# Full-height row loads, a second DMA queue for the first V, and matmuls of zeros at the start of an attention-and-MLP kernel

## The chip, the cores and the metric

The kernel runs on one core of a Trainium2 chip. The metric is the device time of one execution in microseconds (us). The kernel before takes 330.28 us, the median of 5 runs (329.52 to 330.59). One execution of each kernel was taken with a profile: its span (first to last instruction) is about 1.7 us shorter than its device time, and all times of day below are counted from the start of that span.

Engines are named as in the profile: PE multiplies matrices (PEld is its weight load), ACT evaluates functions, DVE and POOL work elementwise, SP only issues DMAs here. POOL and SP each issue DMAs into a queue of their own.

## The reference, cut to what matters

```python
# q, k, v: [B=8, H=8, S=576, D=64] f32
scores = (q @ k.T) / sqrt(D) + slope[h] * -|i - j|       # ALiBi
scores = where((i >= j) & (i - j < 128), scores, -1e9)   # causal window of 128
x = softmax(scores) @ v            # -> x: [B*S = 4608, H*D = 512]
h = x @ w_in                       # w_in:  [512, 2048]
g = h * cos(h)
out = g @ w_out                    # w_out: [2048, 512], out f32
```

The kernel computes in bf16 with f32 accumulation. V, the rows of Q and K, and both weights are f32 in memory. POOL's queue rounds them to bf16 on the way (a casting DMA). What comes through SP's queue in these kernels stays as it is in memory, so V stays f32 there.

## The kernel before

A list scheduler inside the program decides at build time in which order each engine runs its operations; nothing is decided at run time. Batch 0 has a path of its own. Rows of Q and K are loaded in two halves per tensor (`pl` is 0 or 1), transposed by PE through an identity, evicted (copied out of the memory that PE writes) by ACT and DVE; then come pairs of score blocks, exps, a multiplication by a mask that holds window and ALiBi bias, products with V (`pv`), a normalisation, and the first product with w_in for that chunk, with its cosine.

```python
def load_qk(which, src, b, pl):            # two DMAs of 64 partitions each
    fns = []
    for g in range(2):
        fns.append(lambda e, g=g: e.dma_start(
            qB[which][64 * g:64 * g + 64, 2 * pl:2 * pl + 2, :],
            src[b, 4 * g + 2 * pl:4 * g + 2 * pl + 2, :, :].rearrange(
                "h (s j) d -> s h (j d)", j=9)))
    op("pool", fns, w=[("qB", which, pl)], ...)

def load_v(b, order=range(NBLK)):          # NBLK = 5 blocks of up to 128 rows
    for t in order:
        rows = 128 if t < 4 else 64
        op("pool", [lambda e, t=t, rows=rows: e.dma_start(
            vp[b % 2][0:rows, t, :, 0:64],
            v[b, :, 128 * t:128 * t + rows, :].rearrange("h p d -> p h d"))], ...)

# ... the order at the start, which is also POOL's order ...
for pl in range(2):
    load_qk("q", q, 0, pl)
    load_qk("k", k, 0, pl)
    if pl == 0:
        constants()                        # dif, ident: on POOL
load_v(0)
masks()                                    # eight 128x512 exps on ACT
# ... transposes of batch 0 ...
for u in range(4):
    load_w_in(u)                           # 512 of 2048 columns each
for pl in range(2):
    load_qk("q", q, 1, pl)                 # batch 1
    load_qk("k", k, 1, pl)
for u in range(4):
    load_w_out(u)
load_v(1, (3, 4, 0, 1, 2))
attention(0)
```

`r=` and `w=` of an `op` are the data that it reads and writes; the waits follow from them.

The softmax here doesn't subtract the row's maximum and nothing guards it: scores larger than these inputs give would overflow.

Of the kernel before, what the change touches and what calls it, by code (L numbers as in the profile page):

```python
# [34 lines left out]
class Plan:  # L35
# [51 lines left out]

    def schedule(self):
        free = {e: 0 for e in ENG}
        wire = self.WIRE0  # L90
        mode, table = 0, None
        tables = sorted({o.table for o in self.all if o.table is not None})
        left = {t: sum(o.table == t for o in self.all) for t in tables}
        avail = []

        def reach(o, e):
            t = 0
            for d, data in o.preds.items():
                if data == ORDER or self.held(d, data, e):
                    t = max(t, d.start + d.occ)  # L100
                elif d.dma is None and d.eng[0] == e:
                    t = max(t, d.end + 28)
                else:
                    t = max(t, d.end + (53 if e == "pe" else 36))
            return t
        for o in self.all:
            if o.npred == 0:
                avail.append(o)
        order = []
        while avail:  # L110
            phase = next((t for t in tables if left[t]), None)
            best = None
            for e in ENG:
                cand = []
                for o in avail:
                    if e not in o.eng or (o.table is not None and o.table != phase):
                        continue
                    st = max(free[e], reach(o, e))
                    if e == "pe" and o.mode != mode:
                        st += self.SWITCH  # L120
                    cand.append((st, o))
                if not cand:
                    continue
                soon = min(st for st, _ in cand)
                slack = 100 if e == "pe" else 40
                st, o = min(((st, o) for st, o in cand if st <= soon + slack),
                            key=lambda c: (c[1].pri, c[1].seq))
                key = (st, o.pri, o.seq)
                if best is None or key < best[0]:
                    best = (key, e, o)  # L130
            (st, _, _), e, o = best
            avail.remove(o)
            if o.table is not None and o.table != table:
                st += self.TABLE
            if len(o.eng) > 1:
                o.fn, o.occ, o.lat = o.fn[e], o.occ[e], o.lat[e]
                o.eng = (e,)
            o.start = st
            free[e] = st + o.occ
            if o.dma is not None:  # L140
                wire = max(wire, st + 2300) + o.lat
                o.end = max(wire, st + o.occ + 1400) + 500
            else:
                o.end = st + o.lat
            if e == "pe":
                mode = o.mode
            if o.table is not None:
                table = o.table
                left[o.table] -= 1
            order.append(o)  # L150
            for s in o.succs:
                s.npred -= 1
                if s.npred == 0:
                    avail.append(s)
        assert len(order) == len(self.all)
        self.span = max(o.end for o in order)
        self.order = sorted(order, key=lambda o: o.start)
        rank = {id(o): i for i, o in enumerate(order)}
        self.order.sort(key=lambda o: (o.start, rank[id(o)]))
# [81 lines left out]
def bass_alibi_sliding__then__act_gcu_kernel(  # L241
# [8 lines left out]
    with ExitStack() as ctx:  # L250
# [28 lines left out]
        ident = sb("ident", [128, 128])  # L279
        halfpi = sb("halfpi", [128, 1], F32)  # L280
        dif = sb("dif", [128, 2, 128], F32)

        ps = ctx.enter_context(nc.psum_tensor("ps", [128, 8, 512], F32))
        BPE = 2
# [21 lines left out]


        def load_qk(which, src, b, pl):
            fns = []
            for g in range(2):  # L310
                fns.append(lambda e, g=g: e.dma_start(  # L311
                    qB[which][64 * g:64 * g + 64, 2 * pl:2 * pl + 2, :],
                    src[b, 4 * g + 2 * pl:4 * g + 2 * pl + 2, :, :].rearrange(
                        "h (s j) d -> s h (j d)", j=9)))
            op("pool", fns, w=[("qB", which, pl)], dma=f"ld{which}{pl}", occ=1250, lat=1450)

        def load_v(b, order=range(NBLK)):
            for t in order:
# [42 lines left out]

        def constants():
            sel = ["sel"]
            op("pool", lambda e: e.iota(dif[:, :, :], pattern=[[128, 2], [-1, 128]], base=-128,
                                        channel_multiplier=1,
                                        allow_small_or_imprecise_dtypes=True),
               w=["dif"] + sel, occ=350)
            op("pool", lambda e: e.affine_select(
                dif[:, 0, :], dif[:, 0, :], pattern=[[-1, 128]], compare_op=ALU.is_ge,
                fill=-1.0e6, base=-1, channel_multiplier=1), r=["dif"], w=["dif"] + sel, occ=350)  # L370
            op("pool", lambda e: e.affine_select(
                dif[:, 1, :], dif[:, 1, :], pattern=[[1, 128]], compare_op=ALU.is_ge,
                fill=-1.0e6, base=0, channel_multiplier=-1), r=["dif"], w=["dif"] + sel, occ=350)
            op("pool", lambda e: e.memset(ident[:, :], 1.0), w=["ident"] + sel)
            op("pool", lambda e: e.affine_select(
                ident[:, :], ident[:, :], pattern=[[1, 128]], compare_op=ALU.is_equal,
                fill=0.0, base=0, channel_multiplier=-1), r=["ident"], w=["ident"] + sel)
            for i in range(2):
                op("dve", lambda e, i=i: e.memset(vp[i][:, :, :, 64:65], 1.0), w=[("vinit", i)])
                op("dve", lambda e, i=i: e.memset(vp[i][64:128, 4, :, 0:64], 0.0), w=[("vinit", i)])  # L380
                op("dve", lambda e, i=i: e.memset(Pt[i][:, 1024:1088], 0.0), w=[("Pt", i)])
            op("dve", lambda e: e.memset(halfpi[:, :], math.pi / 2.0), w=["halfpi"])
            for i in range(2):
                op("dve", lambda e, i=i: e.memset(
                    tr["k"][i][:, :].rearrange("p (k t) -> p k t", k=NPAIR)[:, :, 576:640], 0.0),
                   w=[("ktail", i)])
# [8 lines left out]
        def masks():  # L395
            for h in range(H):
                op("act", lambda e, h=h: e.activation(
                    EM[:, h, :].rearrange("p (r f) -> p r f", r=2),
                    dif[:, :, :].rearrange("p a b -> p (a b)")[:, None, :].broadcast_to([128, 2, 256]),
                    ACTF.Exp, scale=slopes[h]), r=["dif"], w=[("EM", h)], occ=520, lat=612, table=0)  # L400
            for x in range(2):
                op("dve", lambda e, x=x: e.tensor_copy(
                    EMt[:, 4 * x:4 * x + 4, :].rearrange("p h (n f) -> p h n f", n=2),
# [4 lines left out]
        def qk_transposes(b, which, pl, banks):  # L408
# [5 lines left out]
            def f(e):  # L414
                ins = None
                for n, (j0, j1) in enumerate(jj):
                    for j in range(j0, j1):
                        for x in range(2):
                            ins = e.transpose(  # L419
                                dst(n)[64 * x:64 * x + 64, 128 * (j - j0):128 * (j - j0) + 128],  # L420
                                qB[which][:, 2 * pl + x, 64 * j:64 * j + 64], ident[:, :])
                return ins
            op("pe", f, r=[("qB", which, pl), "ident"], w=[("B", x) for x in banks],
               occ=500, lat=670, mode=2, pri=3)
            for n, (j0, j1) in enumerate(jj):
                o = tr[which][b % 2][:, :].rearrange("p (g l t) -> p g l t", g=2, l=2)[
                    :, :, pl, 0:576].rearrange("p g (s j) -> p g s j", j=9)[:, :, :, j0:j1]
                i = dst(n).rearrange("p (j g s) -> p g s j", j=j1 - j0, g=2)
                op(("act", "dve"),
                   {"act": lambda e, o=o, i=i: e.activation(o, i, ACTF.Copy),  # L430
                    "dve": lambda e, o=o, i=i: e.tensor_copy(o, i)},
# [4 lines left out]
        def tkeys(b, pr=None):  # L436
            if b >= BPE:
                return [("tr", w_, b % 2) for w_ in ("q", "k")] + [("ktail", b % 2)]
            pls = range(2) if pr is None else [pr % 2]
            return [("tr", w_, b % 2, pl, j0) for w_ in ("q", "k") for pl in pls  # L440
                    for j0 in (0, 5)] + [("ktail", b % 2)]


        def units(b):
            if b == 0:
                return [(pr, G) for G in range(2) for pr in (0, 2, 1, 3)] + [("t", None)]
            return [("t", None)] + [(pr, G) for pr in range(NPAIR) for G in range(2)]

        def scores(b, us):
# [265 lines left out]
                    x_back(b, u, n)  # L715


        for pl in range(2):
            load_qk("q", q, 0, pl)
            load_qk("k", k, 0, pl)  # L720
            if pl == 0:
                constants()
        load_v(0)
        masks()
        for pl in range(2):
            for i, which in enumerate(("q", "k")):
                qk_transposes(0, which, pl, (UB, OB)[i])
        for u in range(4):
            load_w_in(u)
        for pl in range(2):  # L730
            load_qk("q", q, 1, pl)
            load_qk("k", k, 1, pl)
# [60 lines left out]
```

## Time and profile before

| | before |
|---|---|
| time, median of 3 | 330.28 us |
| span of the profiled run | 328.4 us |
| PE busy | 311.0 us, 95% |
| first cosine starts | 27.82 |
| second product (with w_out) starts | 43.29 |

The view of busy time by stretch has: from:to, its length, then busy us (and instructions) of PE, PEld, DVE, ACT and POOL, the clock granted to PE, the DMA share and GB/s. For the kernel before:

```profile
0.00:20.00 20.00, 9.74 (x131) 7.03 (x131) 9.15 (x27) 12.12 (x19) 18.39 (x35) 1.00 1.18 139
20.00:40.00 20.00, 19.30 (x251) 15.32 (x249) 17.25 (x40) 16.02 (x23) 16.65 (x21) 1.00 1.23 206
40.00:60.00 20.00, 19.71 (x225) 11.41 (x229) 14.38 (x37) 14.24 (x20) 3.32 (x4) 1.00 2.15 168
60.00:320.00 260.00, 257.24 (x1882) 125.63 (x1917) 157.09 (x339) 168.97 (x251) 62.91 (x75) 1.00 0.82 93
```

Only the first row has room: PE is busy for half of the first 20 us and for 96% or more afterwards. The profile records when PE's clock changes between full (1.00) and half (0.50). A clock of 1.00 in the first rows is not evidence, because the clock record of this run begins only at 24.2; durations have to say it.

The timeline has: start us, duration us, engine, line, operation, output<-inputs, shapes, count, and in brackets how long the engine had been idle and what ended that. PE of the kernel before, its transposes (L419), the pairs of score blocks (L470) and the first product with V (L550):

```profile
9.58 1.17 PE L419 MATMUL ps<-ident,qrows 128*64 128x128 bf16 x18 [1.21 <-DMA qrows<-in_q_dram]
10.69 0.82 PE L470 MATMUL ps<-qt,kt 64*128 64x256 bf16 x8
12.36 1.17 PE L419 MATMUL ps<-ident,krows 128*64 128x128 bf16 x18 [0.86 <-DMA krows<-in_k_dram]
15.01 0.32 PE L550 MATMUL ps<-vp,p 128*128 128x65 bf16 x3 [1.48 <-DVE p L515]
15.44 0.82 PE L470 MATMUL ps<-qt,kt 64*128 64x256 bf16 x8
18.41 1.03 PE L470 MATMUL ps<-qt,kt 64*128 64x256 bf16 x12
22.32 1.04 PE L470 MATMUL ps<-qt,kt 64*128 64x256 bf16 x12
...
33.81 0.69 PE L419 MATMUL ps<-ident,qrows 128*64 128x128 bf16 x18
```

Eighteen transposes take 1.17 us at 9.6 and 0.69 at 33.8: PE is slow in the start. The second pair of scores waits for rows that land at 11 to 12 us. The first product with V, at 15.01, waits for DVE and not for V. POOL's timeline of the kernel before shows why the rows are late:

```profile
2.65 1.21 POOL L311 DMA_DIRECT2D krows<-in_k_dram  x2
3.92 0.40 POOL L364 IOTA dif<- 128x256 f32 x1
...
5.78 1.22 POOL L311 DMA_DIRECT2D qrows<-in_q_dram  x2
6.96 1.23 POOL L311 DMA_DIRECT2D krows<-in_k_dram  x2
8.11 4.31 POOL L320 DMA_DIRECT2D vp<-in_v_dram  x5
12.30 3.09 POOL L350 DMA_DIRECT2D w_inb<-in_moe_w_in_dram  x4
15.25 1.36 POOL L311 DMA_DIRECT2D qrows<-in_q_dram  x2
```

The second half of the rows is issued behind the constants, and V's five loads (4.31 us of issue) stand before the loads of w_in.

### The profile page before, as it was taken

The page shows a single profiled execution, that of the slowest core. Times are in us where ns is not written, and L with a number is a line of the kernel's source. Part 1 is how long each engine was busy: PE and PEld are TensorE (multiplying, and loading weights), DVE is VectorE, ACT ScalarE, POOL GpSimd, SP SyncE. Part 2 cuts the span into 40 slices and gives each one's busy share as a digit, 9 for nine tenths or more (in the row PEclk, how much of TensorE's full clock was granted, in tenths as well). Part 3 has the DMA queues.
Part 4 walks back from the last instruction along what each step waited for, and adds up shares of the span by engine and source line. Part 5 has one row for each costly group of instructions (what it writes and reads, how often), then busy time and mean ns, then how long its engine had stood idle before and what let it go on. Part 6 is the DMA issues. An engine that isn't in the chain of part 4 may idle for free.

```text
span 328.4 us, 6317 instructions
## 1 busy us (share of the span) xinstructions
PE 311.0 (95%) x2504; PEld 161.5 (49%) x2544; DVE 197.9 (60%) x440; ACT 212.6 (65%) x313; POOL 101.3 (31%) x133
## 2 busy tenths in 40 slices
PE   2589999999999999999999999999999999999995
PEld 2367755444544454445444644554455444444442
DVE  2569858585848683969586867576567361254000
ACT  5669768686868585867785788669767663263211
POOL 8999530194572726800780050000000000000000
PEclk9999999999999999999999999999999999999999
DMA  6999999999999999991999395100010000201112
GB/s 89 160 206 204 207 157 177 156 150 151 183 158 153 208 115 162 171 92 52 156 168 105 72 152 39 66 33 2 32 64 2 34 1 32 93 5 64 66 67 93
DMA packets 133918, 35.29 MB, mean 107 GB/s; under 512 B 123136, under 2 KB 129280, under 8 KB 133888
## 3 DMA queue, kind: packets, MB, share of 16 engines
q0 software_dynamic: 100288, 18.36, 70.7%
q1 hardware_dynamic: 33600, 16.52, 21.9%
q8 instruction: 20, 0.33, 0.4%
q14 instruction: 10, 0.08, 0.1%
HBM read 36.70 MB, written 9.44 MB: 141 GB/s over the span
## 4 chain that ended last, share of the span: by engine, by line
PE 89%; DVE 3%; ACT 2%; POOL 2%; issue 2%; DMA 1%; POOLq 0%; ACTq 0%
PE ps L688 37%; PE ps L642 33%; PE ps L665 5%; PE ps L470 5%; PE ps L550 3%; PE ps L614 2%; PE ps L553 2%; DMA krows<-in_k_dram 1%; PE ps L419 1%; DVE p L515 1%; ACT p L500 1%; PE ps L460 1%; POOL qrows L311 1%; PE ps L536 1%; PE ps L538 1%
## 5 line engine op out<-in xcount | busy, mean ns | idle before, releaser
L688 PE MATMUL ps<-w_outb,gT 128*128 128x512 bf16 x548 | 133.4, 379 | 1.9 <-issue 0.6
L642 PE MATMUL ps<-xT,w_inb 128*128 128x512 bf16 x500 | 117.9, 379 | 1.2 <-DVE gT L651 0.4
L651 DVE TENSOR_TENSOR gT<-ps,cos 128x512 bf16<-128x512 f32 x128 | 81.8, 686 | 46.8 <-PE ps L688 29.0
L647 ACT ACTIVATE cos<-ps,halfpi 128x512 f32<-128x512 f32 x128 | 81.8, 689 | 23.0 <-PE ps L688 11.9
L688 PEld LDWEIGHTS ps<-w_outb,gT 128*128 128x128 bf16 x576 | 53.6, 98 | 57.9 <-issue 2.2
L500 ACT ACTIVATE p<-ps 128x768 bf16<-128x768 f32 (+1 forms) x64 | 56.1, 915 | 29.3 <-PE ps L470 29.2
L642 PEld LDWEIGHTS ps<-xT,w_inb 128*128 128x128 bf16 x512 | 46.8, 98 | 55.8 <-DVE gT L651 4.8
L320 POOL DMA_DIRECT2D vp<-in_v_dram x40 | 34.0, 907 | 54.2 <-PE ps L553 46.9
L515 DVE TENSOR_TENSOR p<-p,emask 128x768 bf16<-128x768 bf16 (+1 forms) x64 | 39.1, 613 | 0.2
L694 ACT ACTIVATE ob<-ps 128x512 f32<-128x512 f32 x24 | 14.3, 597 | 33.8 <-PE ps L688 33.8
L330 POOL DMA_DIRECT2D qnat<-in_q_dram x30 | 25.5, 920 | 30.9 <-DMA qt<-qnat 30.9
L330 POOL DMA_DIRECT2D knat<-in_k_dram x30 | 25.6, 926 | 5.4 <-DMA kt<-knat 5.0
L584 DVE TENSOR_TENSOR xnat<-ps,rec 128x256 bf16<-128x256 f32 x64 | 26.6, 418 | 0.7
L628 ACT ACTIVATE xT<-ps 128x256 bf16<-128x256 bf16 (+3 forms) x41 | 14.5, 355 | 18.0 <-PE ps L614 17.9
L550 PE MATMUL ps<-vp,p 128*128 128x65 bf16 x256 | 23.0, 199 | 1.6 <-DVE p L515 1.6
L550 PEld LDWEIGHTS ps<-vp,p 128*128 128x128 bf16 x256 | 17.5, 100 | 11.2 <-issue 4.2
L553 PE MATMUL ps<-vp,p 128*128 128x65 bf16 x192 | 20.7, 197 | 0.0
L470 PE MATMUL ps<-qt,kt 64*128 64x128 bf16 (+1 forms) x320 | 20.6, 253 | 0.0
L696 DVE COPY ob<-ps 128x512 f32<-128x512 f32 x12 | 8.3, 690 | 18.4 <-PE ps L688 18.0
L614 PE MATMUL ps<-ident,xnat 128*128 128x128 bf16 x128 | 18.4, 227 | 0.5 <-DVE xnat L584 0.5
L582 DVE RECIPROCAL rec<-ps 128x4 f32<-128x4 f32 x64 | 11.5, 180 | 11.5 <-PE ps L553 10.4
L665 PE MATMUL ps<-xT,w_inb 128*128 128x256 bf16 x128 | 17.4, 281 | 0.7 <-ACT ptail L492 0.5
(52 smaller groups left out, 201.9 us busy)
## 6 DMA issues: line engine op xcount, KB each, us to landing
out_dram<-ob SPq DMA_DIRECT2D x36, 256.0 KB, 2.0
vp<-in_v_dram POOLq DMA_DIRECT2D x32, 128.0 KB, 8.2
qnat<-in_q_dram POOLq DMA_DIRECT2D x24, 128.0 KB, 6.0
knat<-in_k_dram POOLq DMA_DIRECT2D x24, 128.0 KB, 5.8
w_inb<-in_moe_w_in_dram POOLq DMA_DIRECT2D x4, 512.0 KB, 9.5
w_outb<-in_moe_w_out_dram POOLq DMA_DIRECT2D x4, 512.0 KB, 17.8
qrows<-in_q_dram POOLq DMA_DIRECT2D x8, 144.0 KB, 7.4
krows<-in_k_dram POOLq DMA_DIRECT2D x8, 144.0 KB, 8.2
```

The lines of the kernel that those rows point to most:

```text
L320: op("pool", [lambda e, t=t, rows=rows: e.dma_start(vp[b % 2][0:rows, t, :, 0:64], v[b, :, 128 * t:128 * t + rows, :].rearrange("h p d -> ...
L330: fns.append(lambda e, t=t, rows=rows: e.dma_start(nat[which][0:rows, t, :, :], src[b, :, 128 * t:128 * t + rows, :].rearrange("h p d -> p ...
L470: ins = e.matmul(ps[:, banks[x], c0:c1], keys_ap(b, x, pr, kc), query_ap(b, x, pr, qb, 128 * nb), start=True, stop=True)
L500: op("act", lambda e: e.activation(P[i][:, :, lo:512], src_[:, :, lo:512], ACTF.Exp, scale=0.125), w=held + [("P", i)], occ=920 if u[1] el ...
L515: op("dve", lambda e: e.tensor_tensor(P[i][:, :, lo:512], P[i][:, :, lo:512], EM[:, 2 * pr:2 * pr + 2, lo:512], ALU.mult), r=[("P", i), (" ...
L550: ins = e.matmul(o, P[i][:, x, d0:d0 + 128], V[:, kc, h, 0:65], start=True, stop=not two)
L553: ins = e.matmul(o, P[i][:, x, p0:p0 + 128], V[:, kc - 1, h, 0:65], start=False, stop=True)
L642: op("pe", lambda e, kc=kc: e.matmul(ps[:, bank, :], w_in[:, kc, 128 * fc:128 * fc + 128], xT[:, kc, r0:r0 + CH], start=(kc == 0), stop=(k ...
L647: op("act", lambda e: e.activation(cosb[ci][:, :], ps[:, bank, :], ACTF.Sin, bias=halfpi[:, 0:1]), r=["halfpi"], w=[("B", bank), ("cos", c ...
L651: op("dve", lambda e: e.tensor_tensor(gT[gi][:, fc, :], ps[:, bank, :], cosb[ci][:, :], ALU.mult), r=[("cos", ci)], w=[("B", bank), ("g", ...
L665: op("pe", lambda e, i=i, fc=fc, kc=kc: e.matmul(ps[:, bank, 256 * i:256 * i + 256], w_in[:, kc, 128 * fc:128 * fc + 128], xT[:, kc, r0:r0 ...
L688: op("pe", lambda e, t=t, fc=fc, bank=bank: e.matmul(ps[:, bank, :], gT[gi][:, fc, 128 * t:128 * t + 128], w_out[:, fc, :], start=(fc == 0 ...
```

## The change

The intent is a shorter start. (1) A row load becomes one DMA of 128 partitions, with the parity of the head on the partitions; the transposes become 36 of 64x64 in place of 18 of 128x64. All four row loads go before the constants. (2) V of batch 0 goes to SP's queue, as f32, into a staging area, and POOL rounds it to bf16; the rounding stands behind the issues of w_in in POOL's order. (3) Twelve matmuls of zeros run while the first rows come, so that PE's clock is up. (4) ACT builds the masks at half width and DVE copies the other half.

```diff
 def load_qk(which, src, b, pl):
-    for g in range(2): ... two DMAs of 64 partitions ...
+    op("pool", [lambda e: e.dma_start(
+        qB[which][:, 2 * pl:2 * pl + 2, :],
+        src[b, 4 * pl:4 * pl + 4, :, :].rearrange("(k x) (s j) d -> (x s) k (j d)",
+                                                  x=2, j=9))],
+       w=[("qB", which, pl)], dma=f"ld{which}{pl}", occ=700, lat=1450)
+
+def load_v0():
+    for t in range(NBLK):
+        rows = 128 if t < 4 else 64
+        op("sp", [lambda e, t=t, rows=rows: e.dma_start(
+            vst[0:rows, t, :].rearrange("p (h d) -> p h d", h=H),
+            v[0, :, 128 * t:128 * t + rows, :].rearrange("h p d -> p h d"))],
+           r=[("qB", "k", 0 if t < 2 else 1)], w=[("vst", t)], dma=f"ldf{t}", ...)
+
+def round_v0():
+    for t in range(NBLK):
+        rows = 128 if t < 4 else 64
+        op("pool", lambda e, t=t, rows=rows: e.tensor_copy(
+            vp[0][0:rows, t, :, 0:64], vst[0:rows, t, :]...),
+           r=[("vst", t), ("vinit", 0)], w=[("v", 0, t)], occ=600, lat=700)
 # ... masks: half width on ACT, copies on DVE; ident before dif ...
 # ... transposes: for k_, for x: 64x64 blocks against ident[lo, lo] ...
+op("dve", lambda e: e.memset(zeros[:, :], 0.0), w=["zeros"], pri=0)
+for _ in range(12):
+    op("pe", lambda e: e.matmul(ps[:, 7, :], zeros[:, 0:128], zeros[:, :], ...), ...)
 for pl in range(2):
     load_qk("q", q, 0, pl)
     load_qk("k", k, 0, pl)
-    if pl == 0:
-        constants()
-load_v(0)
+constants()
+load_v0()
 masks()
 # ... transposes ...
 for u in range(4):
     load_w_in(u)
+round_v0()
 for pl in range(2):
     load_qk("q", q, 1, pl)
     load_qk("k", k, 1, pl)
```

The scheduler's model of the transfers changes too: `wire`, the time at which the DMA engines are free, was one number for all queues and is now one for each issuing engine. With the new layout of the rows the order of the head pairs in the score blocks changes as well, and one more wait on the transposes is added.

More of the change, by code (lines that the diff above doesn't have):

```diff
@@ L89, in schedule @@
         free = {e: 0 for e in ENG}
-        wire = self.WIRE0
+        wire = {e: self.WIRE0 for e in ENG}
         mode, table = 0, None
@@ L140, in schedule @@
             if o.dma is not None:
-                wire = max(wire, st + 2300) + o.lat
-                o.end = max(wire, st + o.occ + 1400) + 500
+                wire[e] = max(wire[e], st + 2300) + o.lat
+                o.end = max(wire[e], st + o.occ + 1400) + 500
             else:
@@ L281, in bass_alibi_sliding__then__act_gcu_kernel @@
         dif = sb("dif", [128, 2, 128], F32)
+        zeros = sb("zeros", [128, 512])
+        vst = gT[1][:, :, :].rearrange("p a b -> p (a b)").bitcast(F32)[:, 0:2560].rearrange(
+            "p (t f) -> p t f", t=NBLK)
         ps = ctx.enter_context(nc.psum_tensor("ps", [128, 8, 512], F32))
@@ L308, in load_qk @@
         def load_qk(which, src, b, pl):
-            fns = []
-            for g in range(2):
-                fns.append(lambda e, g=g: e.dma_start(
-                    qB[which][64 * g:64 * g + 64, 2 * pl:2 * pl + 2, :],
-                    src[b, 4 * g + 2 * pl:4 * g + 2 * pl + 2, :, :].rearrange(
-                        "h (s j) d -> s h (j d)", j=9)))
-            op("pool", fns, w=[("qB", which, pl)], dma=f"ld{which}{pl}", occ=1250, lat=1450)
+            op("pool", [lambda e: e.dma_start(
[9 more added lines that the diff above has]
+                    v[0, :, 128 * t:128 * t + rows, :].rearrange("h p d -> p h d"))],
+                   r=[("qB", "k", 0 if t < 2 else 1)], w=[("vst", t)], dma=f"ldf{t}",
+                   occ=350, lat=8 * rows)
+        def round_v0():
+            for t in range(NBLK):
+                rows = 128 if t < 4 else 64
+                op("pool", lambda e, t=t, rows=rows: e.tensor_copy(
+                    vp[0][0:rows, t, :, 0:64],
+                    vst[0:rows, t, :].rearrange("p (h d) -> p h d", h=H)),
+                   r=[("vst", t), ("vinit", 0)], w=[("v", 0, t)], occ=600, lat=700)
         def load_v(b, order=range(NBLK)):
@@ L363, in constants @@
             sel = ["sel"]
+            op("pool", lambda e: e.memset(ident[:, :], 1.0), w=["ident"] + sel)
+            op("pool", lambda e: e.affine_select(
+                ident[:, :], ident[:, :], pattern=[[1, 128]], compare_op=ALU.is_equal,
+                fill=0.0, base=0, channel_multiplier=-1), r=["ident"], w=["ident"] + sel, occ=350)
             op("pool", lambda e: e.iota(dif[:, :, :], pattern=[[128, 2], [-1, 128]], base=-128,
@@ L373, in constants @@
                 fill=-1.0e6, base=0, channel_multiplier=-1), r=["dif"], w=["dif"] + sel, occ=350)
-            op("pool", lambda e: e.memset(ident[:, :], 1.0), w=["ident"] + sel)
-            op("pool", lambda e: e.affine_select(
-                ident[:, :], ident[:, :], pattern=[[1, 128]], compare_op=ALU.is_equal,
-                fill=0.0, base=0, channel_multiplier=-1), r=["ident"], w=["ident"] + sel)
             for i in range(2):
@@ L397, in masks @@
                 op("act", lambda e, h=h: e.activation(
-                    EM[:, h, :].rearrange("p (r f) -> p r f", r=2),
-                    dif[:, :, :].rearrange("p a b -> p (a b)")[:, None, :].broadcast_to([128, 2, 256]),
-                    ACTF.Exp, scale=slopes[h]), r=["dif"], w=[("EM", h)], occ=520, lat=612, table=0)
+                    EM[:, h, 0:256], dif[:, :, :].rearrange("p a b -> p (a b)"),
+                    ACTF.Exp, scale=slopes[h]), r=["dif"], w=[("EM", h)], occ=300, lat=400,
+                   table=0)
+                if h % 2:
+                    op("dve", lambda e, h=h: e.tensor_copy(
+                        EM[:, h - 1:h + 1, 256:512], EM[:, h - 1:h + 1, 0:256]),
+                       r=[("EM", h - 1), ("EM", h)], w=[("EM", h - 1), ("EM", h)],
+                       occ=250, lat=330)
             for x in range(2):
@@ L417, in f @@
                     for j in range(j0, j1):
-                        for x in range(2):
-                            ins = e.transpose(
-                                dst(n)[64 * x:64 * x + 64, 128 * (j - j0):128 * (j - j0) + 128],
-                                qB[which][:, 2 * pl + x, 64 * j:64 * j + 64], ident[:, :])
+                        for k_ in range(2):
+                            for x in range(2):
+                                lo, c0 = slice(64 * x, 64 * x + 64), 128 * (j - j0) + 64 * k_
+                                ins = e.transpose(
+                                    dst(n)[lo, c0:c0 + 64],
+                                    qB[which][lo, 2 * pl + k_, 64 * j:64 * j + 64],
+                                    ident[lo, lo])
                 return ins
@@ L425, in qk_transposes @@
             for n, (j0, j1) in enumerate(jj):
-                o = tr[which][b % 2][:, :].rearrange("p (g l t) -> p g l t", g=2, l=2)[
-                    :, :, pl, 0:576].rearrange("p g (s j) -> p g s j", j=9)[:, :, :, j0:j1]
-                i = dst(n).rearrange("p (j g s) -> p g s j", j=j1 - j0, g=2)
+                o = tr[which][b % 2][:, :].rearrange("p (k t) -> p k t", k=NPAIR)[
+                    :, 2 * pl:2 * pl + 2, 0:576].rearrange("p k (s j) -> p k s j", j=9)[
+                    :, :, :, j0:j1]
+                i = dst(n).rearrange("p (j k s) -> p k s j", j=j1 - j0, k=2)
                 op(("act", "dve"),
@@ L438, in tkeys @@
                 return [("tr", w_, b % 2) for w_ in ("q", "k")] + [("ktail", b % 2)]
-            pls = range(2) if pr is None else [pr % 2]
+            pls = range(2) if pr is None else [pr // 2]
             return [("tr", w_, b % 2, pl, j0) for w_ in ("q", "k") for pl in pls
-                    for j0 in (0, 5)] + [("ktail", b % 2)]
+                    for j0 in (0, 5)] + [("tr", w_, b % 2) for w_ in ("q", "k")] + [
+                        ("ktail", b % 2)]
         def units(b):
             if b == 0:
-                return [(pr, G) for G in range(2) for pr in (0, 2, 1, 3)] + [("t", None)]
+                return [(pr, G) for G in range(2) for pr in range(NPAIR)] + [("t", None)]
             return [("t", None)] + [(pr, G) for pr in range(NPAIR) for G in range(2)]
@@ L715, in attention @@
                     x_back(b, u, n)
+        op("dve", lambda e: e.memset(zeros[:, :], 0.0), w=["zeros"], pri=0)
+        for _ in range(12):
+            op("pe", lambda e: e.matmul(ps[:, 7, :], zeros[:, 0:128], zeros[:, :], start=True,
+                                        stop=True), r=["zeros"], w=[("B", 7)], occ=427, lat=590)
         for pl in range(2):
```

## The prediction

> **What bounds the kernel now.** The page gives PE busy 95% of 328.4 us, and in the chain of waits PE has 89%. From about 27 us on PE is never idle long, so only the start can give anything. There the timeline shows the chain: row loads, transposes, evictions, scores, exps, until the last exp (tail) ends at 26.5, a table load, and the first cosine at 27.8. Then PE, ACT and DVE are all nearly full until the second product starts at 43.0.
>
> In the start three things cost:
> 1. Rows come late. The second pair of row loads is issued only at 5.8 to 8.1, behind the constants; by the landings q lands at 9.5 and k at 12.3, and the second pair of scores starts at 15.4.
> 2. ACT builds eight 128x512 masks, 0.54 each, 4.3 us.
> 3. PE is slow until about 24 to 25: eighteen transposes take 1.17 us against 0.69 later, a 128x256 matmul 0.40 against 0.27, a 12-matmul score pair 1.03. Steps of one score-and-exp pair are 3.9 apart (18.4, 22.3), against 2.6 at 48.8 to 51.4. The Trainium skill, "TensorE: Matmul & The Clock Gate", Part 1, says the clock doubles after roughly 3.4 us of sustained activity; the trace agrees: PE is dense from 18.4 and quickens near 24.
>
> **What the change does.**
> - One row load of 128 partitions instead of two of 64 (0.61 to 0.73 each); I estimate 0.7, so all four are issued by 4.1 instead of 8.1. Transfers ran about 1.7 us per load, so landings near 4.9, 6.6, 8.4, 10.5: k1 about 1.8 earlier.
> - V of batch 0 leaves the POOL queue (4.3 us of issue) for SP, uncast, and POOL rounds it (five copies, estimate 0.6 each). The skill, "DMA: Bandwidth & Descriptors", Issuing engines are not separate DMA queues, says a second queue saves only issue time; so V will share with k1 and w_in. Weights still move up some 2 us.
> - Masks at half width: estimate 0.33 each, 2.6 in all, with four small DVE copies. The mask source is ready at about 5.9 (before 5.2), because the identity goes first and four issues precede it.
> - Twelve zero matmuls from 1.3 to about 6: PE warm before the first transposes. They end when the first rows have landed, so cost nothing.
> - Transposes are 36 of 64x64 instead of 18 of 128x64. Sixteen 64x64 score matmuls take 0.41 warm, so 36 take about 0.9 against 0.62 to 0.69: about +0.25 each, and the four of batch 1 lie in the full stage: +1.0.
>
> **Sum, along ACT's chain.** First scores 10.1 (before 10.7): evictions still stand behind six masks. Second pair 13.2 (15.4). Then warm steps of about 2.6 instead of 3.9: third pair 15.5 to 16, fourth 18.3, tail 21, first cosine about 23.5 (27.8): −4.3. Batch 1's transposes give back 1.0. The rest of the program has the same work and the same waits. Its later data have slack: batch 1 rows land at 28 to 33 for use at 34 to 40; w_out's last piece lands at 43.4, just in time now, and comes about 2 earlier.
>
> Predicted: 327.0 us, range 324.3 to 329.8. Faster by over 2%: 0.07; within 2%: 0.91; slower: 0.02.
>
> **What would show it.** Windows: less PE idle time before 25 us; 128x65 matmuls at 0.19 from the first. First cosine near 23.5, second product near 39.8. Row issues done by 4.1. Transposes of batch 1 at 0.9 each.
>
> **What would make it wrong.** PE falls back or never warms (then about 329). V's uncast packets delay k1, or its rounding makes the first products with V wait (some us). The last w_out piece, still behind the same DMA queue, stalls the second product, so the gain shrinks to about 2. Or transposes cost nothing and steps shrink more: 325.

## The result, and the profile after

The changed kernel takes 339.82 us (median of 5 runs, 339.46 to 339.88). The ratio of its time to before is 1.0289, 95% interval 1.0274 to 1.0305: slower. Here and below a ratio is made from runs of both kernels in one session, so it is not quite the ratio of the medians quoted.

Busy time by stretch of the changed kernel:

```profile
0.00:20.00 20.00, 9.20 (x172) 5.40 (x172) 7.09 (x22) 9.68 (x17) 7.67 (x17) 0.77 0.99 154
20.00:40.00 20.00, 13.01 (x180) 10.24 (x181) 12.33 (x37) 9.98 (x14) 14.08 (x19) 0.72 0.89 148
40.00:60.00 20.00, 19.79 (x307) 13.79 (x308) 13.85 (x25) 14.54 (x20) 11.91 (x15) 1.00 1.91 176
60.00:320.00 260.00, 256.89 (x1944) 126.06 (x1978) 162.44 (x361) 174.63 (x261) 62.90 (x75) 1.00 0.92 96
```

From 20 to 40 us PE did 13.01 us of work in place of 19.30, at a mean clock of 0.72. From 40 us on the rows are alike. So most of the loss lies before 40 us. The view of waits from 0 to 45 us (engine, line, what it waited for: us in total, times, longest) of the changed kernel:

```profile
POOL vp L331 <- DMA gT<-in_v_dram: 16.4, 3, 11.6
...
PE ps L579 <- POOL vp L331: 11.0, 1, 11.0
```

L331 is POOL's rounding and L579 the product with V: PE waits 11.0 us, once, for POOL, and POOL waits for the f32 V (the staging area is in `gT`). The chain that ended last (start us, duration us, what; three "issue" pieces of 0.05 to 0.06 us between these are left out) says the same:

```profile
2.16 6.74 DMA krows<-in_k_dram
8.92 0.45 SPq L322
9.43 16.14 DMA gT<-in_v_dram
25.62 0.62 POOL vp L331
26.29 0.35 PE ps L579 x3
```

One DMA, issued at 9.43, holds the whole kernel until 25.57. Of POOL's timeline after, the issues of w_in, then the rounding, then the rows of batch 1:

```profile
6.36 3.03 POOL L369 DMA_DIRECT2D w_inb<-in_moe_w_in_dram  x4 [0.15 <-issue]
20.95 0.61 POOL L331 CAST vp<-gT 128x512 bf16<-128x512 f32 x1 [11.56 <-DMA gT<-in_v_dram]
25.62 1.37 POOL L331 CAST vp<-gT 128x512 bf16<-128x512 f32 x2 [4.06 <-DMA gT<-in_v_dram]
27.76 1.61 POOL L331 CAST vp<-gT 128x512 bf16<-128x512 f32 x2 [0.77 <-DMA gT<-in_v_dram]
29.32 0.72 POOL L312 DMA_DIRECT2D qrows<-in_q_dram  x1
```

The first copy takes 0.61 us, as was estimated; it is the waiting between copies that costs. In the program's order for POOL the rows of batch 1 stand behind the rounding, so they are issued at 29.32 in place of 15.25. And PE after, its transposes (L445) and score pairs (L499) against those of before:

```profile
5.57 0.76 PE L445 MATMUL ps<-ident,qrows 64*64 64x64 bf16 x36 [0.25 <-DMA qrows<-in_q_dram]
8.95 0.76 PE L445 MATMUL ps<-ident,krows 64*64 64x64 bf16 x36 [2.63 <-DMA krows<-in_k_dram]
...
12.03 1.17 PE L445 MATMUL ps<-ident,krows 64*64 64x64 bf16 x36
14.43 0.82 PE L499 MATMUL ps<-qt,kt 64*128 64x256 bf16 x8 [1.23 <-ACT kt L458]
26.29 0.35 PE L579 MATMUL ps<-vp,p 128*128 128x65 bf16 x3 [11.04 <-POOL vp L331]
...
27.87 1.03 PE L499 MATMUL ps<-qt,kt 64*128 64x256 bf16 x12
```

The second pair does come earlier, 14.43 against 15.44; the third comes at 27.87 against 18.41. The clock record of this run is full from 3.9, half from 10.7, full again from 31.2. The first cosine starts at 35.95 (8.1 later than before), the second product at 52.04 (8.8 later), and the span ends 9.4 later.

Why is V so slow? Each row of V is 64 numbers, 256 bytes as f32. Counting the data packets in the trace's DMA records by queue and size, with the median time that one took, gives this:

| stretch of a run | SP's queue, per us | POOL's queue, per us |
|---|---|---|
| after, 14 to 20 us | V, 256 B: 147 to 165 (31 ns) | w_in, 1024 B: 147 to 155 (96 ns) |
| before, 12 to 14 us | none | V as bf16, 128 B: 1191 to 1208 (32 ns) |

In the changed kernel V and w_in go one packet for one packet. Once w_in has nearly ended, V moves 1007 packets in the us from 24 to 25. A packet of V carries 256 bytes, one of w_in 1024 (bf16; 2048 read). V's share beside w_in is then set by the length of its neighbour's packets. Before, V had the engines nearly to itself and its five blocks landed from 13.17 to 16.92; after, they landed at 20.90, 25.57, 26.32, 27.71 and 27.91, and w_in at 14.84 to 25.07. The first product that waits needs the second block, that is 2048 packets of V. Part of the delay comes before any turns: V was first issued at 8.92, but its first packet moved at 12.74. Why it took so long is not shown. W_in's last piece landed at 25.07, and the V block then in flight within half a us of it.

The Trainium skill, "DMA: Bandwidth & Descriptors", Queues, rings and completion order, says that each DMA engine "round-robins between the queue rows it has work for, at *packet* granularity". The equal counts agree with that. They don't show how many records make up one turn, and in some short stretches of other runs (below) the counts were not equal.

### The profile page after: what moved, and what is told of

Read it like the earlier page. It is cut to its first block, busy times and chain, and to the rows that moved or that the text cites. A ratio compares the mean times of both kernels' runs of the same rounds, so it can differ in the third digit from the quotient of the medians.

```text
span 337.7 us, 6635 instructions
## 1 busy us (share of the span) xinstructions
PE 313.3 (93%) x2660; PEld 161.9 (48%) x2700; DVE 195.7 (58%) x443; ACT 211.8 (63%) x315; POOL 96.6 (29%) x125
## 4 chain that ended last, share of the span: by engine, by line
PE 85%; DMA 7%; DVE 3%; ACT 3%; issue 1%; POOL 0%; SPq 0%; ACTq 0%; POOLq 0%
PE ps L717 35%; PE ps L671 33%; DMA gT<-in_v_dram 5%; PE ps L499 4%; PE ps L694 3%; PE ps L579 3%; PE ps L643 2%; DMA krows<-in_k_dram 2%; PE ps L582 1%; DVE p L544 1%; PE ps L445 1%; PE ps L489 1%; PE ps L565 1%; DVE xnat L613 1%; PE ps L567 1%
## 5 line engine op out<-in xcount | busy, mean ns | idle before, releaser
L339 POOL DMA_DIRECT2D vp<-in_v_dram x35 | 29.8, 900 | 45.5 <-PE ps L582 43.5
L723 ACT ACTIVATE ob<-ps 128x512 f32<-128x512 f32 x29 | 17.3, 596 | 34.5 <-PE ps L717 31.6
L579 PE MATMUL ps<-vp,p 128*128 128x65 bf16 x256 | 22.6, 198 | 11.1 <-POOL vp L331 11.0
L657 ACT ACTIVATE xT<-ps 128x256 bf16<-128x256 bf16 (+3 forms) x38 | 13.4, 354 | 28.8 <-PE ps L643 28.6
L579 PEld LDWEIGHTS ps<-vp,p 128*128 128x128 bf16 x256 | 17.5, 100 | 20.6 <-POOL vp L331 11.4
L499 PE MATMUL ps<-qt,kt 64*128 64x128 bf16 (+1 forms) x320 | 20.3, 250 | 1.2 <-ACT kt L458 1.2
L582 PE MATMUL ps<-vp,p 128*128 128x65 bf16 x192 | 20.2, 195 | 0.0
L499 PEld LDWEIGHTS ps<-qt,kt 64*128 64x128 bf16 x320 | 11.2, 98 | 9.2 <-issue 3.2
```

What stands on the lines that cost most here:

```text
L339: op("pool", [lambda e, t=t, rows=rows: e.dma_start(vp[b % 2][0:rows, t, :, 0:64], v[b, :, 128 * t:128 * t + rows, :].rearrange("h p d -> ...
L499: ins = e.matmul(ps[:, banks[x], c0:c1], keys_ap(b, x, pr, kc), query_ap(b, x, pr, qb, 128 * nb), start=True, stop=True)
L579: ins = e.matmul(o, P[i][:, x, d0:d0 + 128], V[:, kc, h, 0:65], start=True, stop=not two)
```

## The experiments

The theory: V on a second queue takes turns with w_in packet for packet, so its blocks come late; everything else in the change is a small gain. Rivals: the zero matmuls or the many small transposes cost the time; the loss is POOL's rounding work itself; or the half clock makes it.

### V of batch 0 back on POOL's queue, the rest of the change kept

```diff
-        load_v0()
+        load_v(0)
         ...
-        round_v0()
```

> Theory A (V of batch 0 on the second queue is what costs: its 256-byte packets take turns, one for one, with the 1024-byte packets of w_in, so the second block lands at 25.6 us): with V back on the POOL queue and everything else of the change kept, the stall of 11 us before the first products with V is gone, and the time is 324 to 328 us, under the kernel before. Rival B (the single row loads, the small transposes or the zero matmuls cost): the time stays above 333 us.

It took 328.15 us (327.76 to 328.93), ratio to before 0.9941, interval 0.9914 to 0.9969. PE's timeline, L499 being the score pairs:

```profile
14.02 0.82 PE L499 MATMUL ps<-qt,kt 64*128 64x256 bf16 x8 [0.25 <-ACT kt L458]
16.45 1.04 PE L499 MATMUL ps<-qt,kt 64*128 64x256 bf16 x12
20.39 1.04 PE L499 MATMUL ps<-qt,kt 64*128 64x256 bf16 x12
```

The stall is gone and the cosine starts at 25.72, 10.2 earlier than in the changed kernel. The small transposes and the zeros are in this kernel and it is faster than before, so neither is the cause. V landed at 12.23 to 16.26. The clock was full only from 5.0 to 8.4 and then half until 22.1, and the third and fourth pairs are still 3.94 apart, so the gain of 2 us is less than what was predicted.

### Only V's move, put into the kernel before

```diff
-        wire = self.WIRE0
+        wire = {e: self.WIRE0 for e in ENG}      # and its two uses
+        # vst, load_v0(), round_v0() as in the change
-                    for j0 in (0, 5)] + [("ktail", b % 2)]
+                    for j0 in (0, 5)] + [("tr", w_, b % 2) for w_ in ("q", "k")] + [
+                        ("ktail", b % 2)]         # without it the build has a race
-        load_v(0)
+        load_v0()
         ...                                      # after load_w_in:
+        round_v0()
```

> The kernel before with nothing changed but V of batch 0 on the SP queue and rounded by POOL (and one more order of reads and writes that keeps it free of a race). Theory A: the stall appears here too, the first product with V waits until past 24 us, and the time is 336 to 341 us. Rival B: within 2 us of the kernel before.

It took 337.72 us (337.64 to 340.04), ratio 1.0252, interval 1.0213 to 1.0292. The waits of this kernel from 0 to 45 us:

```profile
POOL vp L332 <- DMA gT<-in_v_dram: 15.9, 4, 6.0
...
PE ps L571 <- POOL vp L332: 8.6, 1, 8.6
```

The same wait appears without any zeros or small transposes: V's move alone makes the loss. It is a shorter wait, 8.6 against 11.0. Here w_in is issued from 8.13, behind the slower row loads, and V's first block from 7.76; V still had 646 and 517 packets in the two us from 11 to 13, beside 7 and 73 of w_in. In the changed kernel w_in is issued from 6.36, ahead of V (8.92). The quicker issue of the change thus put w_in in front of V. That is the likely reason why the parts do not add up: this one costs about 8, the rest gains about 2, but together they lose more than 9. No run tests it alone.

### The rounding moved ahead of the issues of w_in

In POOL's order the rounding now stands first, so w_in is issued only when V is in.

```diff
+        round_v0()
         for u in range(4):
             load_w_in(u)
-        round_v0()
```

> The changed kernel with the four w_in issues moved behind POOL's rounding, so that nothing of the POOL queue shares with V once the rows are in. Theory A (sharing with w_in): V's five blocks then move at some 1000 packets a us, as they did after w_in had ended; all have landed by about 17 us and the first product with V starts at 13 to 16 us; w_in in turn comes later, so the time is 326 to 334. Rival C (the second queue is slow by itself with 256-byte packets, or its start is): V still lands after 20 us, and the time is 338 or more.

It took 331.43 us (331.13 to 331.65), ratio 1.0044, interval 1.0021 to 1.0067. V is on the second queue, in f32 and rounded by POOL, as in the changed kernel, and its blocks landed at 12.26 to 16.57; its packets numbered 480 to 996 in each us from 10 to 16, taking 18 ns each. The first product with V no longer waits for it, and the third pair of scores starts at 15.48:

```profile
13.81 0.27 PE L579 MATMUL ps<-vp,p 128*128 128x65 bf16 x3
```

So neither the second queue, nor the longer f32 packets, nor the rounding work is slow as such: w_in beside V is what makes V late. What is lost here is lost later: w_in is issued at 17.30 and lands by 31.20, and the second product starts at 44.29.

### V on SP's queue without waiting for the rows

```diff
-                   r=[("qB", "k", 0 if t < 2 else 1)], w=[("vst", t)], dma=f"ldf{t}",
+                   w=[("vst", t)], dma=f"ldf{t}",
```

> The changed kernel with V issued on the SP queue at once, without waiting for k rows. If packets of two queues take turns one for one (theory A), V's 4608 packets go at the pace of the row packets and then of w_in: about 1000 of them with the rows until 11 us, the rest with w_in, so the second block lands at 16 to 20 us, the rows come 1 to 2 us later than in the changed kernel, and the time is 331 to 336 us. If the fault was only the late issue at 8.9 us, V is there by 12 us and the time is under 328.

It took 330.89 us (330.02 to 331.85), ratio 1.0035, interval 1.0007 to 1.0063. V's first blocks landed at 4.07, 6.53 and 13.44, but the rows came at 7.24, 9.61, 11.45 and 13.29 in place of 5.52, 8.90, 10.35 and 11.84. The expectation missed here: it had the second block at 16 to 20 us and 331 us or more. V moved 678 and 978 packets in the us from 2 to 4, before the rows came, and 928 beside 451 of the rows from 4 to 8, unevenly; that is not one for one. From 8 us on, with about 146 a us beside some 135 of the rows and then 150 of w_in, it again went one for one, and the fourth and fifth blocks landed at 20.09 and 24.66. The first cosine started at 26.20, earlier than before (27.82), but POOL issued w_out only behind the rounding, at 28.39, and PE waited 1.29 for it at 46.2. Going early only changes who pays.

### W_in in pieces of half the width

If turns are by packet and not by byte, shorter w_in packets must give V more. Eight loads of 256 columns have packets of 512 bytes.

```diff
-                w_in[:, :, 512 * u:512 * u + 512], ...
+                w_in[:, :, c:c + 256], ...  for c in (512 * u, 512 * u + 256)
```

> The changed kernel with w_in fetched in eight pieces of 256 columns instead of four of 512, so that its packets are 512 bytes instead of 1024. If the queues take turns packet for packet (theory A), V's rate beside w_in rises from 150 to some 200 to 280 packets a us, the second block lands at 18 to 22 us instead of 25.6, and the time falls to 333 to 337. If they share by bytes, V's rate and the time stay as in the changed kernel.

It took 337.59 us (336.98 to 339.12), ratio 1.0243, interval 1.0216 to 1.027. From 14 to 20 us the trace counts 232 to 249 packets of V a us beside 226 to 241 of w_in, 59 ns each. Again they go one for one, now faster. V's second block landed at 20.67 in place of 25.57. Of these 4.9 us some 2 can come from V's earlier start in this execution (first packet at 10.75 against 12.74, because K's first rows landed earlier and V was issued at 7.21 instead of 8.92); the rates do not depend on that. The waits from 0 to 45 us:

```profile
POOL vp L331 <- DMA gT<-in_v_dram: 14.6, 4, 4.0
...
PE ps L580 <- POOL vp L331: 9.4, 2, 7.2
```

The wait split in two, the longer 7.2 us: w_in itself got slower (it landed by 28.7), so the later V blocks came later, and the time stayed just above the 333 to 337 expected. The rate is the dose that the theory asks for. Of the rivals, none has the size of w_in's packets in it.

### V on POOL's queue, and no zeros

```diff
-        op("dve", lambda e: e.memset(zeros[:, :], 0.0), w=["zeros"], pri=0)
-        for _ in range(12):
-            op("pe", lambda e: e.matmul(ps[:, 7, :], zeros[:, 0:128], zeros[:, :], ...
```

> As the first run, with V on the POOL queue, and without the twelve zero matmuls and their memset. In the changed kernel the clock record is at half from 11.0 us on in spite of them. If the clock falls back there too (theory D), the zeros buy only faster transposes and the two runs differ by less than 0.7 us; if the clock stays up with V back (the prediction's step), this run is 2 to 4 us slower than the first.

It took 329.18 us (328.74 to 329.51), ratio 0.9976, interval 0.9951 to 1.0. The zeros are thus worth about 1.0 us (328.15 against 329.18 in the same session; the two intervals overlap), a little gain rather than a cost. That lies between the two cases of the expectation, nearer to theory D. (The expectation's 11.0 for the changed kernel is 10.7 in its clock record.) The clock record goes up for good at 24.0 here and at 22.1 with zeros, less than one step (3.4 us) of that record apart. With zeros it was up once before, from 5.0 to 8.4, and fell back. The twelve zeros do not keep it up by themselves.

### More matmuls of zeros between the stages

Groups of zero matmuls are put where PE would be idle: six after the first transposes of Q, three after those of K, two and four after the second ones, three after the second and third score pairs. V is on POOL's queue.

```diff
+                if b == 0:      # inside the transposes
+                    for _ in range({("q", 0): 6, ("k", 0): 3, ("q", 1): 2}.get((which, pl), 0)):
+                        e.matmul(ps[:, 7, :], zeros[:, 0:128], zeros[:, :], ...)
 ...
+                if b == 0 and g == 0:        # in attention(0)
+                    fill(4, 3, ("fill", 0, "k", 1))
+                if b == 0 and g in (2, 4):
+                    fill(3, 0, ("S", 0, g))
```

> V on the POOL queue as in the first run, and more zero matmuls (21 beside the first 12) in the waits of PE up to the third pair of scores, on banks that nothing reads then. The prediction said that a warm PE makes a score-and-exp pair take 2.6 us instead of 3.9. If that step was right and only the keeping warm failed, the clock stays full from about 5 us on, the third and fourth pairs of scores start 2.5 to 3 us apart, and the time is 1.5 to 3 us under the first run's: 325 to 326.7 us. If ACT or the waits set the pairs anyway, the time stays within 0.7 us of the first run's.

It took 327.15 us (326.8 to 329.12, 6 runs), ratio 0.9927, interval 0.9904 to 0.995. It has the lowest ratio here. The clock record is full from its first entry near 6 on. PE's timeline, L503 being the score pairs here:

```profile
16.11 0.62 PE L503 MATMUL ps<-qt,kt 64*128 64x256 bf16 x12 [0.56 <-ACT p L541]
...
18.77 0.61 PE L503 MATMUL ps<-qt,kt 64*128 64x256 bf16 x12
```

The steps of the prediction are there: a 12-matmul pair takes 0.62, the pairs are 2.66 apart, the cosine starts at 23.66. The gain in time over the kernel without fillers is 0.5 (by the ratios, 0.9927 against 0.9941, whose intervals overlap) to 1 us (by the medians, of two sessions). So the steps came as expected and the time did not: 325 to 326.7 was expected. Of the 4.2 us by which the cosine starts earlier than before (23.66 against 27.82) the time keeps some 2.4; where the rest goes was not tested. Its profiled execution was the slowest of its six (329.12; the other five took 326.80 to 327.26) and PE stood still in it for 2.01 us at 32.9, which the profile puts down to nothing but "issue"; so that gap seems to belong to that execution and not to the kernel.

### The fillers without the last two groups

```diff
-                if b == 0 and g in (2, 4):
-                    fill(3, 0, ("S", 0, g))
```

> The filled kernel without the two groups of three zero matmuls after the second and third pairs of scores. If those were needed to hold the clock, the record falls to half between 8 and 22 again, score pairs are 3.9 apart and the time is 328 or more. If the earlier fillers were enough, the clock stays full, the first cosine is near 23.2 and the time is 327.2 or a little less. Of the 2.01 us PE gap near 33: if it comes from instruction fetch by a PE that runs ahead, it stays when PE is as early as in the filled kernel and is gone when PE is later; if it was an accident of that one execution, it is gone in both.

It took 327.46 us (327.1 to 328.35, 6 runs), ratio 0.9932, interval 0.9915 to 0.9949: the same as with all groups. The clock stayed full, the cosine starts at 24.03 and the second product at 39.93. There is no gap at 33 although PE is as early, nor in the filled kernel with the gate below, which agrees with an accident of one execution. The cause of that gap stays open.

### V's issue held back until the first rows of K are in, without and with fillers

In the runs above the first K rows landed late (8.90 after, 8.22 with V back), with three of the sixteen DMA engines finishing well behind the others in the changed kernel. POOL was issuing other loads then. The test holds V's loads back.

```diff
-                   r=[("vinit", b % 2)], ...
+                   r=[("vinit", b % 2)] + ([("qB", "k", 0)] if b == 0 else []), ...
```

> As the first run, but POOL issues V only when the first k rows have landed[...]. In the run with w_in late POOL was idle then, and the first k rows landed at 6.9 us; in the others, where POOL issued from 6.35 on, the last of the 16 engines brought them at 7.9 to 8.9. If POOL's issuing is what holds up the stragglers, k lands by 7.1 here and the first scores start 0.5 to 1 us earlier; if it is chance, k lands anywhere from 6.9 to 8.9. Time 327 to 328.3 us.

> The filled kernel (V of batch 0 back on the casting queue, extra zero matmuls between the stages) with V's loads waiting for the first k rows. If the late k rows came from issuing V while rows are in flight (k rows 6.99 with the gate, 7.2 to 8.9 without), k lands by 7.0, the first scores start near 10.2, the first cosine near 22.9, and the time is about 326.5 or less. If the start is no longer what limits because of a gap of PE that moves about near 33, the first cosine comes earlier and the time stays at 327 to 328. If V then comes too late for the first product, a wait on V before 14 us shows and the gain is lost.

Without fillers it took 329.41 us (328.0 to 330.36, 6 runs), ratio 0.9987, interval 0.9963 to 1.0011. With fillers it took 328.09 us (327.42 to 328.99, 6 runs), ratio 0.9945, interval 0.9929 to 0.9961. K's first rows landed at 6.99 and 7.02, and at 6.94 in the kernel with w_in late: POOL was idle in these three. In the kernels that go on issuing from 6.35 they landed at 7.20 to 8.90. This is an association in nine traces (those of this V order or of V behind w_in); how an issue would delay a transfer already under way was not shown. And it does not pay. Without fillers the time lies above the 328.3 expected, and the profiled execution was the fastest of the six (328.0), so it does not show what made the others slower. With fillers the last case of the expectation came: with the gate the score pairs start at 10.45, but PE then waits for V:

```profile
14.50 0.25 PE L592 MATMUL ps<-vp,p 128*128 128x65 bf16 x3 [1.77 <-DMA vp<-in_v_dram]
```

## Why the prediction was wrong, point by point

- **The step that failed** is the first product with V. The prediction cited that a second queue saves only issue time, and went on: "so V will share with k1 and w_in". It put no number on that share. It named late products with V only as a risk of "some us". The wait is 11.0 us, and undoing V's move takes 11.7 us off the time (339.82 to 328.15, in two sessions). The cost could have been estimated from what lay before the reader: w_in moved about 200 packets a us at 16 to 18 us of the kernel before, and the change holds V back until K's rows are in, while w_in waits for no rows. If V gets one packet for each of w_in's, the 2048 packets of its first two blocks take 10 us or more. The prediction counted issue time and a time per load, and the unit that mattered was the packet.
- **"Third pair 15.5 to 16"**, "fourth 18.3", "first cosine about 23.5": 27.87, 30.94 and 35.95, all behind that one wait. With V back and fillers they are 16.11, 18.77 and 23.66, so the mechanism of these steps was right and its condition was not met.
- **Row landings "near 4.9, 6.6, 8.4, 10.5"**: 5.52, 8.90, 10.35, 11.84. The issues were done by 4.3 (predicted 4.1); the transfers were later by 0.6 to 2.3. First scores were predicted at 10.1 and came at 11.28, the second pair at 13.2 and came at 14.43.
- **Zeros make "PE warm before the first transposes"**: the first two groups of 36 took 0.76 in the changed kernel, so it was warm, but it did not last: the record is half from 10.7, and the fourth group took 1.17. "PE falls back" was listed as a risk. It is worth 0.5 to 1 us (the kernel with fillers against the one without, near the noise) and explains nothing of the loss, since the kernel with V back has the half clock too.
- **Transposes "about +0.25 each"**: 0.76 against 0.69 at full clock, so +0.07 each, +0.3 for the four of batch 1 in place of +1.0. This term was mis-sized.
- **"The rest of the program has the same work and the same waits"** was right after 60 us: from there to 320 PE was busy 256.89 against 257.24. Before that it was not quite: the loss grew from 8.1 us at the first cosine to 9.4 at the end.
- **w_out "comes about 2 earlier"**: it came by 49.9 in place of 43.4, because POOL, which issues it, was held by the rounding.
- The 327.0 us predicted for the whole is what the kernel with V back and fillers takes, 327.15. This agreement is in part luck: the transposes cost 0.7 less than predicted, and of the cosine's 4.2 us the time kept only some 2.4. It does not excuse the term left out.

## What to carry to other kernels

When a load moves to a second DMA queue, ask what its packets will stand beside: here the queues went packet for packet, so short packets beside 1024-byte ones advanced at 150 a us where they had gone at 480 to 1007 alone. Before moving it, find the instruction that needs the first bytes, and hold back the bulk transfer that nobody needs yet, or keep the order in one queue. A gain in the issue of a transfer that is not urgent can be a loss, because it gets in front of one that is.

## What the Trainium skill lacked or had wrong

- "DMA: Bandwidth & Descriptors", Issuing engines are not separate DMA queues, says that issuing from several engines "will only save the time on the sequencer". It lacks that a load may get much slower by it: V's five blocks were in 8.8 us after their first issue before (8.11 to 16.92), and 19.0 us after it in the changed kernel (8.92 to 27.91).
- The same page, Queues, rings and completion order, has the turns by packet; it lacks what follows for the rate. Measured: 147 to 165 packets of 256 B a us beside 147 to 155 of 1024 B, and 232 to 249 beside 226 to 241 of 512 B. It speaks of 9 to 17 descriptors in a packet; these counts do not tell the length of a turn.
- The same page, Latency and other measured facts, gives about 0.6 us to the first byte for a load issued by SP. Beside a loaded POOL queue V's first packet came at 12.7, 3.8 us after its issue at 8.92 began. In the kernel that issues V at once it came at 1.93, 1.1 us after the issue began and 0.7 after it ended, so there the figure agrees.
- "TensorE: Matmul & The Clock Gate", Part 1, has the clock fall after at least one idle window of about 3.4 us. The clock records here do move in steps of 3.41 us, but the clock fell seven times in the first 25 us of these kernels, each time after a step in which PE was busy for 0.32 to 0.59 of the time (0.32 in the changed kernel, 0.50 with V back, 0.48 with w_in late, 0.59 with the gate alone, 0.33 and 0.59 with V first, 0.45 with short w_in), never after an idle one (no idle step occurred at full clock). It stayed up after every step of 0.61 or more; between 0.47 and 0.59 both happened. It came back after steps of 0.88 to 1.00, though one of 0.88, with w_in late, did not bring it back.
- The same page, Part 4, says that transposes don't count as PE-busy in the same way. The traces here speak against it, if these transposes run in the mode that the page means (they are listed as MATMUL): the kernel with w_in late kept its clock through a step with 0.55 busy, of which only 0.11 was other matmuls, and in the kernel with V first the clock came back at 14.5 after a step with 0.88 busy, of which 0.24 was other matmuls. In the changed kernel the step before the fall at 10.7 held nothing but transposes, but these filled only 0.32 of it, so it settles nothing.
- No page was found to say that POOL issuing further loads goes with later landing of those under way (first K rows 7.20 to 8.90 with, 6.94 to 7.02 without). It is seen and not explained.
